# An attention and MLP mixer on one core: a second queue for one load, w4 products moved between units, and softmax sums sent by DMA instead of TensorE

## The chip, the core and the metric

The kernel runs on one core of a Trainium2 chip. A core has TensorE (PE, matrix products into PSUM), VectorE (DVE), ScalarE (ACT), GpSimd (POOL) and SyncE (SP), each with an instruction stream of its own that runs in order; they wait for each other by semaphores. DMAs are issued from the streams of SP, ACT and POOL. The metric is device time in microseconds of one execution. Times of the kernel before, three runs: 198.87, 199.20 and 199.33 us, median 199.2.

## What is computed

The input x has 2048 positions of 512 features. It is layer-normed, and two branches are formed from it:

```
xn = layernorm(x)
# A: attention, 32 heads of 16; position i looks at i, i-2, ..., i-14 (8 keys, step 2)
q, k, v = split(xn @ wqkv);  s = softmax(q.k / 4 over the 8 keys) . v  @ wo
# B: gated mixer
h  = gelu(layernorm(xn) @ w1);  hs = (h, four quarters shifted by 1, -1, 2, -2 positions) @ w2
x1 = xn + hs;  h2 = gelu(layernorm(x1) @ w3) @ w4       # w3: 512 x 1376
out = x + s * silu(x1 + h2)
```

All tensors are bf16, sums are taken in f32.

## The kernel before, in words

Since the keys of a position lie at even distances, even and odd positions never meet in the attention. They are kept as two halves, p = 0 and 1, of 1024 positions each, and each half is cut into 8 output tiles of 128 positions; tiles are numbered 0 to 15 over both.

**Front part (to about 103 us).** x is loaded in tiles of 128 positions (load_x, L115), normed on DVE and transposed, and q, k (qk, L283), w1, w2 and w3 follow for four chunks of 512 positions. The first loads are issued on SP in this order: x tiles 0 and 1, half of wqk, x tiles 2 and 3, the other half of wqk, then larger pieces of x.

**Units.** Attention is done in 17 units (list `order`, numbers 0 to 16). Unit 0 takes the first 64 positions of both halves, every other unit 128 keys and 112 to 120 queries of one half: units 1 to 8 half 0, units 9 to 16 half 1. A unit has these steps:
- scores (L593): 32 small products into the four PSUM banks "s";
- exps (L609): ACT takes the exponential of the whole score block, 128 x 2048;
- within (L617): DVE takes the minimum with a band of 0 and huge values, which clears what lies outside the 8 keys;
- weighted (L636), one unit later: 64 small products with the values, into the two banks "o". The values tile carries a constant 2.0 beside each head, so the rows of o_ps also hold twice the sum of the weights. DVE copies and adds the strip that the two blocks of 64 share (mix, L666, L667), and an eviction (ACT, L668) writes the rest to orw;
- values (L568): 4 products for the next unit into bank "b", evicted by ACT.

**w4 products.** Between these, TensorE multiplies h3 by w4, 11 products for each of the 16 tiles, into bank "w" (w4_part, L522). DVE adds x1 to the sum (L537). The gate is then made as x * (1 + tanh(x/2)), which is twice the silu: tanh on ACT (gate_tanh, L550), product on DVE (gate_mult, L558). Near the end the ACT table of Silu is loaded instead (L922), and gate_silu (L544) makes the gate in one step; the factor 2, which the doubled sums need, then comes in the final multiply.

**Sums.** Units are grouped in runs (L60): one unit, or two neighbours. The outputs of a run must be divided by its sums and brought from orw to the layout oT that the last product needs. There are two ways:
- by DMA: sums_gather (two DMAs on SP put the sums on 128 partitions), sums_invert (DVE reciprocal, then a DMA to DRAM), sums_read (a DMA that spreads them over all partitions, into orw), sums_apply (a multiply of oT). moves (L684) are eight DMAs, one for each group of heads, that carry orw to oT on SP's and POOL's queues;
- by TensorE: sums_turn (8 products, L703), sums_inverse (DVE reciprocal and two ACT copies), sums_back (4 products, L741), sums_mult (DVE, L750), and for the moves rows (8 products, L728, and an ACT copy).

Runs here are (0), (1,2), (3,4), ..., (11,12), (13), (14), (15), (16); the last three, 14, 15 and 16, go by TensorE (the moves of 14 by DMA).

**Output.** final (L789) multiplies oT of one tile with wo, 4 products into a bank (often "b", the one of values); a gate multiply on DVE (L813, L811) and an add of x follow (POOL, L818), and store (L843) writes two tiles. Tiles 0 to 7 of half 0 and tiles 0 and 1 of half 1 are done in units 6 to 15, the other six after the loop, the last two partly by TensorE (pe_add, L831).

**What sets the order.** Every engine's instructions stand in the order of the source: the last lines of the kernel bind each instruction to the one before it on its engine. So the order of the loop (L855 to L916) and of the lines after it (L917 to L961) is the order on each engine and queue. PSUM has eight banks; in the loop "s" holds four, "o" two, "w" and "b" one each, and after the loop the four of "s" become "f", "g", "h", "i".

Of the kernel before, what the change touches and what calls it, by code (L numbers as in the profile page):

```python
# [8 lines left out]
AF = mybir.ActivationFunctionType  # L9
# [6 lines left out]
def kernel(  # L16
# [19 lines left out]
    W = 8  # L36
    F = 1376
    ND = D // P
    NF = (F + P - 1) // P
# [3 lines left out]
    CH = 512  # L43
# [15 lines left out]
    NC = 3  # L59
    runs = [(0, 0)] + [(a, a + 1) for a in range(1, NN - NC - 1, 2)] + [(a, a) for a in range(NN - NC - 1, NN)]  # L60

# [53 lines left out]
    def load_x(c, n):  # L115
        p, k = c // 2, c % 2
        for t0 in range(k * TPC, (k + 1) * TPC, n):
            sp.dma_start(  # L118
                out=xn[p][:, t0 : t0 + n, :],
                in_=xv[p, t0 * P : (t0 + n) * P, :].rearrange("(i q) d -> q i d", q=P),  # L120
            )
            yield
# [513 lines left out]
    def weighted(n, first=lambda: None):  # L636
# [27 lines left out]
        first()  # L664
# [3 lines left out]
        return lambda: act.activation(wide(ow, c, KB, m), wide(ov_, 0, CH + W, m), AF.Copy)  # L668
# [83 lines left out]
    def sums_invert(i):  # L752
        _, a, b, _, rw, parts = run_of(runs[i][0])
        dn = rden[i]
        rb = small.tile([P, H * rw // P], BF16, name="rb", tag="rb")
        with nc.allow_low_precision("bf16 weights"):
            dve.reciprocal(out=rb, in_=dn)
        rden_d = dram.tile([8, ND * rw], BF16, name=f"rden_d{i}")
        sp.dma_start(out=rden_d.rearrange("h (a m) -> (h a) m", a=P // 8), in_=rb)
        rden[i] = rden_d  # L760
# [89 lines left out]
    CUT = 6  # L850
# [4 lines left out]
    for n in range(NN - 1):  # L855
        scores(n)
        back = [i for i, (a, b) in enumerate(runs) if b == n - 2 and i < R - NC]
        done = [i for i, (a, b) in enumerate(runs) if b == n - 1]
        evict = weighted(n - 1) if n > 0 else lambda: None
        for i in back:  # L860
            sums_invert(i)
        exps(n, 2 if n == 0 else 1)
        if n == NN - 2:
            values(n + 1)
        evict()
        if 0 < n < NN - 2:
            values(n + 1)
        gate_mult()
        if n < NN - 2:
            gate_tanh()  # L870
        for i in done:
            if i < R - NC:
                sums_gather(i)
        if n == 2:
            moves(0, [sp, pool], 1)
        for i in back:
            if 0 < i < R - NC - 1:
                moves(i, [sp], None, [6, 7])
            sums_read(i)
        for i in done:  # L880
            if i == 0:
                moves(i, [sp, pool], 0)
            elif i < R - NC - 1:
                moves(i, [pool, sp], None, range(6))
            elif i == R - NC - 1:
                moves(i, [pool], None, range(4))
            else:
                moves(i, [pool, sp])
        if n == NN - 2:
            store(sp, 0, 6)  # L890
        within(n, 2 if n == 0 else 1)
        late = [i for i, (a, b) in enumerate(runs) if n == max(b + 3, 5)]
        w4_part(n, 0, NF if n < NN - 2 else CUT)
        if n == 0:
            values(n + 1)
        gate = final(*final_at[n]) if n in final_at else None
        if n == NN - 2:
            banks["end"] = True
            sums_turn(R - 3, "o")
            sums_inverse(R - 3)  # L900
            for i in late:
                sums_apply(i)
        if gate:
            gate(pool)
        if n < NN - 2:
            for i in late:
                sums_apply(i)
        if n == NN - 3:
            moves(R - NC - 1, [pool], None, range(4, 8))
        if n % 2 == 0 and 10 <= n < NN - 3:  # L910
            load_xo((n - 2) // 8, (n - 2) % 8)
        if n - 1 in final_at and n % 2 == 0 and n < NN - 3:
            p, i = final_at[n - 1]
            store(sp, p, i - 1)
        if n in (10, 12):
            load_xo(1, n - 6)  # L916
    scores(NN - 1)  # L917
    evict = weighted(NN - 2)
    store(sp, 1, 0)
    exps(NN - 1)  # L920
    evict()
    act.preload_act_table_set("silu_and_others")  # L922
    w4_part(NN - 2, CUT, NF)
    gate_silu(NN - 2)
    within(NN - 1)
    gate2 = final(1, 2, "b")
    layout("high", f=1, g=1, h=1, i=1)
    sums_back(R - 3, "f")
    gate3 = final(1, 3, "h")
    sums_apply(R - 4, pool)  # L930
    evict = weighted(NN - 1, first=lambda: gate2(pool))
    evict()
    sums_turn(R - 2, "g")
    sums_inverse(R - 2, rows(R - 2, "i"), True)
    gate3(pool)
    store(sp, 1, 2)
    gate4 = final(1, 4, "w")
    sums_mult(R - 3)
    sums_turn(R - 1, "g")
    sums_back(R - 2, "f")  # L940
    sums_inverse(R - 1, rows(R - 1, "h"), True)
    sums_mult(R - 2)
    gate_silu(NN - 3)
    gate5 = final(1, 5, "b")
# [3 lines left out]
    sums_back(R - 1, "i")  # L948
    gate6 = final(1, 6, "g")
    sums_mult(R - 1)  # L950
# [3 lines left out]
    gate7 = final(1, 7, "fw", lambda: add6(gate6.sg))  # L954
# [47 lines left out]
```

## Time and profile before

| | us |
|---|---|
| median of three runs | 199.2 |
| profiled execution, its own time | 199.36 |
| span from first to last instruction in it | 197.6 |
| TensorE busy | 190.2 |
| ScalarE busy | 126.7 |
| VectorE busy | 125.1 |
| GpSimd busy | 61.8 |
| mean DMA rate | 113 GB/s |

The granted TensorE clock is 1.0 throughout. A busy TensorE is not one at its peak, since products overlap. In the timeline each line gives the start and the length in us, the engine, the line of the kernel, the operation, what it writes and reads, and how many were merged; a bracket tells how long the engine stood idle before and what released it. SPq is the issuing of DMAs by SP, PEld the loading of weights. A DMA's line is its issue; when its data has landed is seen only from who waits for it.

### The profile page before, as it was taken

To read this page: it belongs to the slowest core of one execution; us is meant where nothing else is said; L and a number is where in the kernel's file an instruction comes from. 1 tells how busy PE (TensorE), PEld (TensorE's weight loads), DVE (VectorE), ACT (ScalarE), POOL (GpSimd) and SP (SyncE) were. 2 spreads that over 40 slices of the span, in tenths; PEclk is the share of its full clock that TensorE was granted. 3 is DMA by queue.
4 is the path that set the end of the run, shared out by engine and by line. 5 is a ranking of instruction groups with operands and counts; after the bars stand their busy time and mean duration, and the time that the engine had idled before them with its cause. 6 is when DMAs were issued, how large, how long until landed. Compare 5 with 4: busy or idle time off the path is not lost.

```text
span 197.6 us, 6164 instructions
## 1 busy us (share of the span) xinstructions
PE 190.2 (96%) x2591; PEld 98.5 (50%) x2591; DVE 125.1 (63%) x249; ACT 126.7 (64%) x140; POOL 61.8 (31%) x114
## 2 busy tenths in 40 slices
PE   7699999999999999999999999999999999999991
PEld 2588844444444444444444555555555554546550
DVE  4788856418539968200004776788888887786892
ACT  3559849644830643556558788887666676667961
POOL 4135722810200220200000533032626242469760
PEclk9999999999999999999999999999999999999999
DMA  5982181389452256460330012222232271713333
GB/s 158 304 281 84 60 268 53 122 151 339 140 154 62 76 137 167 121 140 0 119 117 3 12 22 66 73 49 69 44 101 62 59 207 31 233 33 88 88 119 108
DMA packets 33643, 22.32 MB, mean 113 GB/s; under 512 B 17584, under 2 KB 33104, under 8 KB 33616
## 3 DMA queue, kind: packets, MB, share of 16 engines
q1 hardware_dynamic: 32256, 21.06, 37.5%
q0 software_dynamic: 1216, 0.81, 2.1%
q8 instruction: 20, 0.33, 0.7%
q10 hardware_dynamic: 144, 0.07, 0.1%
q14 instruction: 7, 0.06, 0.1%
HBM read 12.41 MB, written 4.83 MB: 87 GB/s over the span
## 4 chain that ended last, share of the span: by engine, by line
PE 91%; DMA 3%; DVE 2%; SPq 1%; issue 1%; ACT 1%; DVEq 0%
PE w_ps L529 19%; PE w_ps L394 18%; PE qk_ps L297 13%; PE v_ps L582 8%; PE w_ps L354 7%; PE w_ps L330 7%; PE wo_ps L802 6%; PE o_ps L650 6%; DMA wqk_sb<-in_A_wqkv_dram 3%; PE s_ps L603 3%; PE w_ps L410 1%; PE tr_ps L265 1%; SPq L118 1%; PE dt_ps L703 1%; DVE oT L750 1%
## 5 line engine op out<-in xcount | busy, mean ns | idle before, releaser
L614 ACT ACTIVATE prob<-s_ps 128x2048 bf16<-128x2048 f32 (+1 forms) x18 | 31.9, 1781 | 18.0 <-PE s_ps L603 17.9
L529 PE MATMUL w_ps<-w_sb,h3T 128*128 128x512 bf16 (+1 forms) x176 | 40.8, 379 | 0.0
L398 ACT ACTIVATE h3T<-w_ps 128x1024 bf16<-128x1024 f32 x20 | 20.5, 1023 | 24.9 <-PE w_ps L394 24.9
L693 POOL DMA_DIRECT2D oT<-orw x38 | 19.4, 518 | 49.9 <-DVE orw L658 30.3
L394 PE MATMUL w_ps<-x1nT,w_sb 128*128 128x512 bf16 x160 | 35.0, 379 | 0.0
L297 PE MATMUL qk_ps<-xnT,wqk_sb 128*128 128x256 bf16 (+1 forms) x192 | 29.7, 308 | 1.2 <-DMA wqk_sb<-in_A_wqkv_dram 0.7
L529 PEld LDWEIGHTS <-h3T 128*128 128x128 bf16 (+1 forms) x176 | 17.1, 98 | 20.4
L394 PEld LDWEIGHTS <-w_sb 128*128 128x128 bf16 x160 | 15.6, 98 | 19.1 <-issue 0.4
L297 PEld LDWEIGHTS <-wqk_sb 128*128 128x128 bf16 x192 | 18.3, 98 | 11.2 <-DMA wqk_sb<-in_A_wqkv_dram 1.0
L623 DVE TENSOR_TENSOR prob<-prob,band 128x2048 bf16<-128x2048 bf16 (+1 forms) x18 | 21.0, 1167 | 2.9 <-ACT prob L614 2.7
L304 ACT ACTIVATE qT<-qk_ps,sel 128x1024 bf16<-128x1024 f32 x16 | 16.7, 1113 | 6.6 <-PE qk_ps L297 6.5
L818 POOL TENSOR_TENSOR xo<-sg,xo 128x512 bf16<-128x512 bf16 x9 | 11.7, 1304 | 21.5 <-DVE sg L813 21.5
L802 PE MATMUL wo_ps<-wo_sb,oT 128*128 128x512 bf16 (+1 forms) x68 | 16.6, 366 | 0.1
L582 PE MATMUL v_ps<-wv_sb,xnT 128*128 128x512 bf16 x64 | 16.6, 381 | 0.0
L359 DVE TENSOR_TENSOR xn<-w_ps,xn 128x1024 bf16<-128x1024 f32 x8 | 9.7, 1212 | 10.6 <-PE w_ps L354 10.6
L537 DVE TENSOR_TENSOR xn<-w_ps,xn 128x512 bf16<-128x512 f32 x15 | 10.4, 691 | 7.6 <-PE w_ps L529 7.5
L585 DVE CAST v_aug<-v_ps 128x512 bf16<-128x512 f32 x1 | 0.7, 691 | 22.5 <-ACT h3T L398 22.5
L668 ACT ACTIVATE orw<-o_ps 128x896 bf16<-128x896 f32 x16 | 14.6, 913 | 0.1
L330 PE MATMUL w_ps<-xn2T,w_sb 128*128 128x512 bf16 x64 | 14.5, 379 | 0.0
L354 PE MATMUL w_ps<-w_sb,hT 128*128 128x512 bf16 x64 | 14.3, 379 | 0.0
L650 PE MATMUL o_ps<-prob,v_aug 64*32 64x64 bf16 x1088 | 12.2, 195 | 0.1
L334 ACT ACTIVATE hT<-w_ps 128x1024 bf16<-128x1024 f32 x8 | 8.2, 1028 | 6.2 <-PE w_ps L330 6.2
(100 smaller groups left out, 236.0 us busy)
## 6 DMA issues: line engine op xcount, KB each, us to landing
x1n_dram<-xn SPq DMA_DIRECT2D x4, 512.0 KB
xn<-in_A_x_dram SPq DMA_DIRECT2D x6, 256.0 KB
xo<-in_A_x_dram SPq DMA_DIRECT2D x6, 256.0 KB
out_dram<-xo SPq DMA_DIRECT2D x6, 256.0 KB
orw<-rden_d SPq DMA_DIRECT2D x6, 240.0 KB
w_sb<-in_B_w_dram SPq DMA_DIRECT2D x1, 1376.0 KB
w_sb<-in_B_w_dram SPq DMA_DIRECT2D x1, 1280.0 KB
wqk_sb<-in_A_wqkv_dram SPq DMA_DIRECT2D x2, 512.0 KB
```

Source lines behind the costliest of these rows:

```text
L297: pe.matmul(pt[:, b, :], lhsT=wqk_sb[:, dt, nt * P : (nt + 1) * P], rhs=xnT[p][:, dt, ms], start=(dt == 0), stop=(dt == ND - 1),)
L330: pe.matmul(pt[:, b, :], lhsT=w1_sb[:, dt, g * P : (g + 1) * P], rhs=xn2T[:, dt, :], start=(dt == 0), stop=(dt == ND - 1),)
L354: pe.matmul(pt[:, j, :], lhsT=w2_src(p, g, m0), rhs=w2_sb[:, g, :], start=(g == 0), stop=(g == ND - 1),)
L394: pe.matmul(pt[:, b, :], lhsT=w3_sb[:, dt, ft * P : (ft + 1) * P], rhs=x1nT[:, dt, :], start=(dt == 0), stop=(dt == ND - 1),)
L398: act.activation(h3_tile(c)[:, 2 * a : 2 * a + 2, :], pt, AF.Gelu_apprx_tanh)
L529: pe.matmul(pt, lhsT=h3[c][:fs, ft, jj * P : (jj + 1) * P], rhs=w4_sb[:fs, ft, :], start=(ft == 0), stop=(ft == NF - 1 and t < NN - 2),)
L582: pe.matmul(vp, lhsT=xnT[p][:, dt, k0 : k0 + P], rhs=wv_sb[:, dt, :], start=first, stop=last)
L614: act.activation(pr[:, rs_], t[:, rs_], AF.Exp, scale=SCALE)
L623: dve.tensor_tensor(out=w, in0=w, in1=b.unsqueeze(1).to_broadcast([P, m, KB]), op=ALU.min)
L650: pe.matmul(op[32 * cg : 32 * cg + 32, s, g * KB : (g + 1) * KB], lhsT=va[KB * s : KB * s + KB, dt * 8 + h, :], rhs=pr[KB * s : KB * s + K ...
L693: queues[hh % len(queues)].dma_start(out=oT[p][DH * hh : DH * (hh + 1), :, q0 : q0 + nq], in_=w[32 * cg : 32 * cg + DH, ND * jj : ND * jj ...
L802: pe.matmul(pt, lhsT=oT[p][:, dt, i * P : (i + 1) * P], rhs=wo_sb[:, dt, cs], start=(dt == 0), stop=(dt == ND - 1),)
```

## The change

Five things change together.
1. x tile 1 is issued by ACT's queue instead of SP's.
2. Units 1 to 6 take 7 or 8 w4 products each instead of 11; a tile may begin in one unit and end in the next. Units 7 to 15 take the whole tile n - 2. Tiles 14 and 15 are multiplied after the loop, tile 15 in bank "f". Tiles 12, 13 and 14 get their gate by Silu (before, tile 14 alone); tile 15 as before.
3. Runs are now (0), (1,2), ..., (13,14), (15), (16), and only run 16 goes by TensorE. Run 15's moves are issued after the loop, five on POOL and three on SP.
4. The eviction of o_ps of unit 15 is done by DVE instead of ACT.
5. In units up to 6 the reciprocal, the last two moves and the read of a run stand behind within; sums_apply of runs 0 and 1 stands ahead of within in unit 6 (before, behind the w4 products of unit 5).

```diff
-    NC = 3
-    runs = [(0, 0)] + [(a, a + 1) for a in range(1, NN - NC - 1, 2)] + [(a, a) for a in range(NN - NC - 1, NN)]
+    runs = [(0, 0)] + [(a, a + 1) for a in range(1, NN - 2, 2)] + [(a, a) for a in range(NN - 2, NN)]
...
-            sp.dma_start(
+            (act if (c, t0) == (0, 1) else sp).dma_start(
...
-        return lambda: act.activation(wide(ow, c, KB, m), wide(ov_, 0, CH + W, m), AF.Copy)
+        dst, src = wide(ow, c, KB, m), wide(ov_, 0, CH + W, m)
+        return lambda: act.activation(dst, src, AF.Copy) if eng is act else eng.tensor_copy(out=dst, in_=src)
...
+    part = {0: [(0, 0, NF)]}
+    for n in (1, 4):
+        t = 1 + (n - 1) // 3 * 2
+        part.update({n: [(t, 0, 7)], n + 1: [(t, 7, NF), (t + 1, 0, 3)], n + 2: [(t + 1, 3, NF)]})
+    part.update({n: [(n - 2, 0, NF)] for n in range(7, NN - 1)})
...
         evict = weighted(n - 1) if n > 0 else lambda: None
-        for i in back:
-            sums_invert(i)
+        if n > 6:
+            for i in back:
+                sums_invert(i)
         exps(n, 2 if n == 0 else 1)
...
         evict()
-        if 0 < n < NN - 2:
-            values(n + 1)
         gate_mult()
+        if len(part[n]) > 1:
+            w4_part(*part[n][0])
+        if n > 0:
+            values(n + 1)
...
+        if n == 6:
+            sums_apply(0)
+            sums_apply(1)
         within(n, 2 if n == 0 else 1)
+        if n <= 6:
+            for i in back:
+                sums_invert(i)
+            read_back()
...
-        w4_part(n, 0, NF if n < NN - 2 else CUT)
+        w4_part(*part[n][-1])
...
     scores(NN - 1)
-    evict = weighted(NN - 2)
-    store(sp, 1, 0)
+    evict = weighted(NN - 2, dve)
+    sums_invert(R - 3)
     exps(NN - 1)
     evict()
+    sums_gather(R - 2)
+    sums_read(R - 3)
+    moves(R - 2, [pool], None, range(5))
     act.preload_act_table_set("silu_and_others")
-    w4_part(NN - 2, CUT, NF)
-    gate_silu(NN - 2)
-    within(NN - 1)
-    gate2 = final(1, 2, "b")
-    layout("high", f=1, g=1, h=1, i=1)
-    sums_back(R - 3, "f")
-    gate3 = final(1, 3, "h")
-    sums_apply(R - 4, pool)
-    evict = weighted(NN - 1, first=lambda: gate2(pool))
-    evict()
-    sums_turn(R - 2, "g")
-    sums_inverse(R - 2, rows(R - 2, "i"), True)
-    gate3(pool)
-    store(sp, 1, 2)
-    gate4 = final(1, 4, "w")
-    sums_mult(R - 3)
-    sums_turn(R - 1, "g")
-    sums_back(R - 2, "f")
-    sums_inverse(R - 1, rows(R - 1, "h"), True)
-    sums_mult(R - 2)
-    gate_silu(NN - 3)
-    gate5 = final(1, 5, "b")
+    gate_mult()
+    within(NN - 1)
+    w4_part(NN - 3, 0, NF)
+    for t in range(NN - 5, NN - 2):
+        gate_silu(t)
+    gate2 = final(1, 2, "b")
+    gate2(pool)
+    sums_invert(R - 2)
+    moves(R - 2, [sp], None, range(5, 8))
+    sums_read(R - 2)
+    store(sp, 1, 0)
+    evict = weighted(NN - 1)
+    evict()
+    sums_apply(R - 3)
+    layout("high", f=1, g=1, h=1, i=1)
+    w4_part(NN - 2, 0, NF, "f")
+    gate_silu(NN - 2)
+    sums_turn(R - 1, "g")
+    sums_inverse(R - 1, rows(R - 1, "i"), True)
+    gate3 = final(1, 3, "b")
+    sums_back(R - 1, "g")
+    gate3(pool)
+    store(sp, 1, 2)
+    gate4 = final(1, 4, "h")
+    sums_mult(R - 1)
+    sums_apply(R - 2)
+    gate5 = final(1, 5, "w")
     gate4(pool)
     gate5(pool)
     store(sp, 1, 4)
-    sums_back(R - 1, "i")
-    gate6 = final(1, 6, "g")
-    sums_mult(R - 1)
+    gate6 = final(1, 6, "b")
```

Here R is the number of runs and NN = 17 that of units, so R - 1 is the run of unit 16, and after the change R - 2 is run 15 and R - 3 run (13,14). In the text "run 14" or "run 15" names a run by its unit.

## The prediction

> **What bounds the kernel now.** I read the engines' busy time first, then the chain that ended last, then the timeline of its three stretches: start, one attention unit, tail.
>
> ```profile
> PE 190.2 (96%) x2591; PEld 98.5 (50%) x2591; DVE 125.1 (63%) x249; ACT 126.7 (64%) x140; POOL 61.8 (31%) x114
> PE 91%; DMA 3%; DVE 2%; SPq 1%; issue 1%; ACT 1%; DVEq 0%
> ```
>
> TensorE is the chain from 9.29 us to about 193 us. Its work counts in full wherever it stands; moving it gains only where it fills a hole, and costs where it opens one. The timeline of the start, and of one early unit:
>
> ```profile
> 0.80 0.86 SPq L118 DMA_DIRECT2D xn<-in_A_x_dram  x2
> 1.70 0.43 SPq L128 DMA_DIRECT2D wqk_sb<-in_A_wqkv_dram  x1
> 9.29 1.05 PE L297 MATMUL qk_ps<-xnT,wqk_sb 128*128 128x256 bf16 x8 [0.74 <-DMA wqk_sb<-in_A_wqkv_dram]
> ...
> 116.84 0.43 PE L603 MATMUL s_ps<-qT,kT 32*64 32x128 bf16 x32
> 117.20 0.75 PE L650 MATMUL o_ps<-prob,v_aug 64*32 64x64 bf16 x64
> 117.37 1.88 ACT L614 ACTIVATE prob<-s_ps 128x2048 bf16<-128x2048 f32 x1 [0.61 <-PE s_ps L603]
> 118.04 0.22 DVE L666 COPY mix<-o_ps 128x64 f32<-128x64 f32 x1 [0.40 <-PE o_ps L650]
> 118.44 0.68 DVE L561 SCALAR_TENSOR_TENSOR xn<-sig,xn 128x512 bf16<-128x512 bf16 x1
> 119.28 1.23 DVE L623 TENSOR_TENSOR prob<-prob,band 128x2048 bf16<-128x2048 bf16 x1 [0.16 <-ACT prob L614]
> ```
>
> Scores start a unit; exps begin 0.55 us later and last 1.88, the band minimum follows with 1.22, and only then may the next unit's o_ps run. That is 3.7 us of latency inside a unit of 4.3, so it is hidden now, by 0.6 us. The tail:
>
> ```profile
> 181.54 0.43 PE L603 MATMUL s_ps<-qT,kT 32*64 32x128 bf16 x32
> 182.66 0.65 SPq L765 DMA_DIRECT2D orw<-rden_d  x1
> 183.36 2.61 SPq L693 DMA_DIRECT2D oT<-orw  x4
> 185.64 1.25 POOL L773 TENSOR_TENSOR oT<-oT,orw 128x480 bf16<-128x480 bf16 x1 [0.78 <-DMA orw<-rden_d]
> 189.99 1.35 DVE L813 TENSOR_TENSOR slots<-wo_ps,xn 128x512 bf16<-128x512 f32 x2
> 190.80 2.27 POOL L818 TENSOR_TENSOR slots<-slots 128x512 bf16<-128x512 bf16 x2 [1.40 <-PE wo_ps L802]
> 193.10 1.68 SPq L844 DMA_DIRECT2D out_dram<-slots  x3
> ```
>
> The reader should see that a read of reciprocals from DRAM takes 2.95 us from issue to use, and that the end is carried by the gates of output tiles 4 and 5: multiply at 189.99 on DVE, two adds on POOL, three stores on SP. I take A = the scores of unit 16 (181.54) and G = the multiply of gate 4 (189.99 = A + 8.45) as marks; from G to the span's end are 7.65 us.
>
> **The change, part by part, up to A.**
>
> *x tile 1.* SP issues x 0, x 1, wqk half 0 at 0.80, 1.25, 1.70; without x 1 all that follows is issued 0.45 earlier. The DMA share stays at 0.75 or more from 2.0 us nearly throughout to 13.5 (windows of 0.5 us), so the stream moves as a block and wqk half 1 lands 0.45 earlier, inside the 0.74 that TensorE waits. Tile 0 now shares the engines with tile 1 and can land up to 0.37 later (128 KB at about 350 GB/s); its chain to the first qk matmul then ends near 8.9 instead of 8.55. ScalarE's table load moves back by one issue, 0.45, to 2.5; its first root is at 3.94. Bounds 0 and -0.45; I take **-0.40**, nearer the issue slot, since no other wait follows on TensorE before 103 us.
>
> *Products moved behind A.* Before A stood 15 whole w4 tiles and 6 products, 171; now 14 tiles, 154. Eleven products take 2.38 us: 17 x 0.216 = **-3.68**, to come back in the tail. sums_turn of run 14 also leaves this stretch: **-0.41** (chain, L703 at 181.21).
>
> *Holes in units 1 to 6.* A unit shrinks to 0.36 + 0.61 + 0.97 + 7 x 0.216 = 3.45 us (3.67 with 8). ScalarE needs 1.77 + 0.80 + 0.48 + 0.53 = 3.58 with a tanh and 3.05 without (the steps between its starts at 113.07, 114.84, 115.64 and 116.12, and a tanh of 0.64 less an overlap of 0.11); four of six have one, so its mean of 3.40 just fits. DVE does not always. In units 2 and 5 one w4 tile ends and the next begins in the same PSUM bank, with only values (0.97) between. Measured from the scores: the mix copy at 1.31, gate_mult at 1.71, the w4 add at about 2.30 to 2.99 (0.69, L537); TensorE is ready for the new tile at 2.80 and starts at 3.06: 0.26. The band minimum follows the add, 2.91 to 4.13; o_ps wants to start at 4.07: 0.13. Twice 0.39 is **+0.78**. Units 1, 3 and 4 come out with 0.01 to 0.5 to spare.
>
> *Unit 7.* sums_apply of runs 0 and 1 now stands before the band minimum of unit 6 (1.07 us as at 130.73), which ends at 4.77 after that unit's scores. Behind it wait the reciprocal (0.44), the w4 add (0.61) and the first gate's multiply (0.69), so the multiply ends 1.75 us after unit 7's scores. values(8) needs that multiply's bank ("b") at 0.97 and starts at 1.82: **+0.85**. Before, this multiply stood at 135.30, 0.12 behind the scores, and ended in time. Nothing before shows either kind of hole; the low end is 0 for both (DVE's gaps smaller than its issue steps), the high end twice (a gate_mult beside POOL's add took 1.06 at 136.71 instead of 0.63).
>
> A therefore comes at 181.54 - 0.40 - 3.68 - 0.41 + 0.78 + 0.85 = **178.68**.
>
> **From A to G**, times counted from A. DVE: multiply 0.18, apply 0.78, mix 1.35, its add 1.60 (as unit 14 before: scores 171.75, then 171.93, 172.53, 173.10, 173.35), reciprocal of run (13,14) 1.74, then the copy of o_ps that ScalarE did: 1.07 long (L658's 1.225 x 896/1024), 2.18 to 3.25. Next on DVE the band minimum to 4.47; o_ps(16), wanted at 4.21, waits 0.33. Then the w4(14) add and gate 2, to 5.69.
>
> Run 15's sums start from that copy: two gathers on SP 3.28 to 4.5 (1.23 at 175.11). Landing after the issue: between 1.4 (moves on POOL's queue, 1.9 with 0.51 of issue) and 3.2 (issue end 170.87, reciprocal released 174.1, behind x loads); one at 121.25 was in by 122.94, so I take 1.4, no loads being ahead: 5.9. Reciprocal to 6.28, write issued to 6.8, three moves at 0.65 ahead of the read in SP's queue to 8.75, read at 8.8, landing 2.95 later: 11.75. sums_apply (half of 0.65) 11.8 to 12.15. Gate 4 stands behind it on DVE: **G = A + 12.15**, against 8.45. Its own wo_ps is ready at 10.97.
>
> TensorE in the meantime: w4(14) to 3.35, final(1,2) to 4.21, o_ps(16) to 5.15, w4(15) with its identity product to 7.75, turn and rows of run 16 to 8.55, final(1,3) to 9.4, a hole to 9.9 (the reciprocal on DVE waits behind the apply of run (13,14), whose 240 KB read, issued at 4.55, is in after 3.5; data of the one at 177.91 moved until 180.8), back, final(1,4) and (1,5) to 11.83. The 22 products thus fill the first 8 us, and the sums of two runs that no longer pass through TensorE (0.41 + 0.54 + 2 x 0.21 + 0.33 = 1.70 us) are not missed: SP's loop ends last. The mix copy of unit 16 waits behind the DMA-fed reciprocal (6.3), and ScalarE's eviction behind it ends at 7.75, just when TensorE asks. ScalarE's table load and three Silu (1.28 + 3 x 0.6) end by 5.8, before that eviction at 6.85.
>
> Past G the order is the old one (gates 4, 5 on DVE, POOL, three stores), so 7.65 stays; final(1,6) waits to 12.2 and the last ScalarE store falls at 15.4, before SP's last.
>
> The Trainium skill, "DMA: Bandwidth & Descriptors", section "Anatomy of one DMA", gives about 2.0 us plus bytes/436e3 per us for a GpSimd-issued DMA: 2.28 for a read of this size (an estimate from that page). The read above took 2.95, with a queue behind it; by the page's figure the sum would be 199.4 instead of 200.0.
>
> **Sum.** G = 178.68 + 12.15 = 190.83, 0.84 later than 189.99. The profiled execution took 199.36 (span 197.6 and 1.7 around it): 200.2, and it lies 0.16 above the median of the runs: **200.0**.
>
> **Rivals.**
> - *Loop lands sooner.* If the read is in by A + 11.1, DVE is just done with the multiply of run 16 (11.0) and G falls 0.65 earlier: about 199.35. For it: part of the 2.95 may be the four moves queued behind that read. Against: the windows show its data moving only 1.3 to 2.35 us after issue. The skill's 2.0 us leans this way.
> - *No holes in the loop (faster).* If DVE's order leaves units 2, 5 and 7 unharmed, 1.63 us return: 198.4. It turns faster than before once the holes are under 0.4 together. For it: DVE shows 1 to 2 us idle per unit now. Against: the idle is not where the waits fall.
> - *More holes.* If band minimum and exps bind each of the six short units (they have 0.1 us of slack, and POOL's work stretches DVE's), 0.2 to 0.3 each: 201.3.
> - *x tile 1 gains nothing* (wqk half 1 is bound by the stream): 200.4, inside my case.
>
> **Numbers.** Forecast case 0.45 (199.65 to 200.8), sooner 0.17, no holes 0.18, more holes 0.20. About 0.2%, 0.4 us, is what a measurement of this kernel can tell. The no-hole case gives faster, with a little of the sooner case: 0.21; same: most of the sooner case and the forecast's low edge, 0.19; slower 0.60. Range 198.6 to 201.3.
>
> **What the profile after would show.** TensorE's wait for wqk gone or under 0.3 us; PE idle on DVE at the third products of units 2 and 5 and at values in unit 7; A near 178.7; the reciprocal of run 15 waiting for its gather; DVE idle before its last sums_apply, released by the DMA orw<-rden_d; G near 190.8. I am wrong if A is below 178 (holes absent), or if the last apply doesn't wait.

## The result, and the profile after

The changed kernel takes 204.52 us (median of 5 executions, 202.97 to 205.05) against 199.2 us before: a ratio of 1.026, 95% interval 1.022 to 1.031. It is slower by 5.3 us, where 0.8 us had been forecast; 204.5 lies far above the range of 198.6 to 201.3. The profiled execution took 204.8, with a span of 203.1 us (before: 197.6).

The page of the changed kernel, engines' busy time and the chain that ended last:

```profile
PE 190.5 (94%) x2533; PEld 97.7 (48%) x2559; DVE 124.1 (61%) x247; ACT 124.5 (61%) x134; POOL 59.2 (29%) x110
PE 70%; DMA 10%; DVE 6%; ACT 5%; issue 3%; SPq 3%; ACTq 0%
```

TensorE is busy for as long as before, though it has 1.7 us less to do, and its share of the chain has fallen from 91% to 70%. DMA has gone from 3% to 10%. The kernel has stopped being one long row of products. Two stretches of the timeline show where. The first is units 6 and 7 of the changed kernel (start, length, engine, line, operation, and in brackets the idle time before it and what ended that):

```profile
126.21 0.64 SPq L765 DMA_DIRECT2D orw<-rden_d  x1
126.42 0.43 PE L603 MATMUL s_ps<-qT,kT 32*64 32x128 bf16 x32
...
130.39 0.66 DVE L773 TENSOR_TENSOR oT<-oT,orw 128x960 bf16<-128x960 bf16 x1 [1.00 <-DMA oT<-orw]
130.97 1.22 DVE L623 TENSOR_TENSOR prob<-prob,band 128x2048 bf16<-128x2048 bf16 x1
131.11 1.04 PE L802 MATMUL wo_ps<-wo_sb,oT 128*128 128x512 bf16 x4 [0.77 <-DVE oT L773]
132.08 0.43 PE L603 MATMUL s_ps<-qT,kT 32*64 32x128 bf16 x32
...
133.82 1.02 PE L582 MATMUL v_ps<-wv_sb,xnT 128*128 128x512 bf16 x3 [0.70 <-DVE sg L813]
```

The read of run (1,2)'s reciprocals is issued at 126.21 and its multiply runs 4.18 us later, after DVE has waited 1.00 us. final(0,0) waits behind it. At 133.82 is the wait in unit 7 that the prediction had named. The second stretch is the tail:

```profile
180.46 0.43 PE L603 MATMUL s_ps<-qT,kT 32*64 32x128 bf16 x32
185.25 0.61 SPq L765 DMA_DIRECT2D orw<-rden_d  x1
187.09 2.94 SPq L693 DMA_DIRECT2D oT<-orw  x3
190.64 0.66 DVE L773 TENSOR_TENSOR oT<-oT,orw 128x960 bf16<-128x960 bf16 x1 [3.61 <-DMA oT<-orw]
190.76 0.64 SPq L765 DMA_DIRECT2D orw<-rden_d  x1
192.37 0.38 PE L741 MATMUL rr_ps<-ident,slots 120*128 120x120 bf16 x4 [2.28 <-ACT slots L716]
192.81 4.44 PE L802 MATMUL wo_ps<-wo_sb,oT 128*128 128x512 bf16 x12
192.86 0.66 DVE L750 TENSOR_TENSOR oT<-rr_ps,oT 128x480 bf16<-128x480 f32 x1 [0.75 <-ACT oT L733]
194.04 0.41 DVE L773 TENSOR_TENSOR oT<-oT,orw 128x480 bf16<-128x480 bf16 x1 [0.52 <-DMA orw<-rden_d]
194.51 0.69 DVE L811 SCALAR_TENSOR_TENSOR slots<-wo_ps,xn 128x512 bf16<-128x512 f32 x1
196.22 0.69 DVE L811 SCALAR_TENSOR_TENSOR slots<-wo_ps,xn 128x512 bf16<-128x512 f32 x1 [1.01 <-PE wo_ps L802]
```

The multiply of run (13,14) keeps DVE waiting for 3.61 us; it runs 5.39 us after its read was issued. Run 16's reciprocal stands behind it on DVE, and TensorE needs that one for sums_back, so TensorE stands for 2.3 us. Only behind sums_back come the multiply of run 16 (192.86) and run 15's (194.04). The 12 products after the hole take 4.44 us instead of 2.6. The windows of the changed kernel say why (columns: stretch, its length, busy time of PE, PEld, DVE, ACT, POOL with instruction counts, then the granted TensorE clock, the DMA share and GB/s):

```profile
193.00:194.00 1.00, 1.00 (x4) 0.41 (x3) 0.52 (x1) 0.00 (x0) 0.34 (x1) 0.52 0.59 203
194.00:195.00 1.00, 1.00 (x4) 0.29 (x2) 0.89 (x2) 0.00 (x0) 0.00 (x0) 0.50 0.68 245
195.00:196.00 1.00, 1.00 (x4) 0.31 (x3) 0.21 (x1) 0.00 (x0) 0.71 (x1) 0.50 0.06 17
196.00:197.00 1.00, 1.00 (x5) 0.45 (x4) 0.69 (x1) 0.00 (x0) 0.44 (x2) 0.78 0.00 0
```

The granted clock is 0.50 for 3.4 us: from about 193.04 (0.52 in its window) to 196.44 (0.78 in its window). Before, it was 1.0 throughout.

The marks A (scores of unit 16), G (the multiply of gate 4) and the end give the sum:

| | before | forecast | after |
|---|---|---|---|
| scores of unit 1 | 108.21 | 107.81 | 107.92 |
| A | 181.54 | 178.68 | 180.46 |
| A to G | 8.45 | 12.15 | 14.05 |
| G to end of span | 7.65 | 7.65 | 8.6 |
| span | 197.6 | 198.5 | 203.1 |

As a ledger of the 5.5 us: unit 1 begins 0.29 earlier, and the sums taken from TensorE give -1.70 (0.41 of it before A); new waits before A cost +3.30 (A would stand at 177.16 without them: 181.54 - 0.29 - 3.68 - 0.41), and the tail costs +4.16. The tail, and unit 6 before A, have one thing in common: DVE waits for a transfer, and TensorE for DVE. The experiments test how much of the loss that is.

### The profile page after: what moved, and what is told of

It reads as the page before. It is cut to its first block, busy times and chain, and to the rows that moved or that the text cites. A ratio compares the mean times of both kernels' runs of the same rounds, so it can differ in the third digit from the quotient of the medians.

```text
span 203.1 us, 6062 instructions
## 1 busy us (share of the span) xinstructions
PE 190.5 (94%) x2533; PEld 97.7 (48%) x2559; DVE 124.1 (61%) x247; ACT 124.5 (61%) x134; POOL 59.2 (29%) x110
## 4 chain that ended last, share of the span: by engine, by line
PE 70%; DMA 10%; DVE 6%; ACT 5%; issue 3%; SPq 3%; ACTq 0%
PE w_ps L394 17%; PE qk_ps L297 14%; PE w_ps L529 8%; PE w_ps L354 7%; PE w_ps L330 7%; DMA oT<-orw 5%; PE wo_ps L802 5%; PE v_ps L582 5%; PE o_ps L650 3%; SPq L679 2%; ACT orw L668 2%; PE s_ps L603 2%; DMA dn<-orw 2%; DMA rden_d<-rb 2%; ACT v_aug L587 2%
## 5 line engine op out<-in xcount | busy, mean ns | idle before, releaser
L398 ACT ACTIVATE h3T<-w_ps 128x1024 bf16<-128x1024 f32 x20 | 20.5, 1023 | 24.9 <-PE w_ps L394 24.9
L693 POOL DMA_DIRECT2D oT<-orw x35 | 17.9, 519 | 47.8 <-DVE orw L658 30.3
L529 PEld LDWEIGHTS <-h3T 128*128 128x128 bf16 (+1 forms) x176 | 16.8, 98 | 20.6 <-issue 0.9
L623 DVE TENSOR_TENSOR prob<-prob,band 128x2048 bf16<-128x2048 bf16 (+1 forms) x18 | 21.1, 1173 | 3.4 <-ACT prob L614 3.4
L818 POOL TENSOR_TENSOR xo<-sg,xo 128x512 bf16<-128x512 bf16 x10 | 12.9, 1289 | 27.6 <-DVE sg L813 27.6
L304 ACT ACTIVATE qT<-qk_ps,sel 128x1024 bf16<-128x1024 f32 x16 | 16.7, 1112 | 6.6 <-PE qk_ps L297 6.5
L802 PE MATMUL wo_ps<-wo_sb,oT 128*128 128x512 bf16 (+1 forms) x68 | 18.0, 396 | 1.0 <-DVE oT L773 0.8
L582 PE MATMUL v_ps<-wv_sb,xnT 128*128 128x512 bf16 x51 | 15.9, 381 | 1.4 <-DVE sg L813 0.7
L668 ACT ACTIVATE orw<-o_ps 128x896 bf16<-128x896 f32 x15 | 13.7, 913 | 1.8 <-DVE orw L666 1.8
L650 PE MATMUL o_ps<-prob,v_aug 64*32 64x64 bf16 x1088 | 12.9, 196 | 0.0
```

What stands on the lines that cost most here:

```text
L398: act.activation(h3_tile(c)[:, 2 * a : 2 * a + 2, :], pt, AF.Gelu_apprx_tanh)
L529: pe.matmul(pt, lhsT=h3[c][:fs, ft, jj * P : (jj + 1) * P], rhs=w4_sb[:fs, ft, :], start=(ft == 0), stop=(ft == NF - 1 and t < NN - 2),)
L582: pe.matmul(vp, lhsT=xnT[p][:, dt, k0 : k0 + P], rhs=wv_sb[:, dt, :], start=first, stop=last)
L623: dve.tensor_tensor(out=w, in0=w, in1=b.unsqueeze(1).to_broadcast([P, m, KB]), op=ALU.min)
L650: pe.matmul(op[32 * cg : 32 * cg + 32, s, g * KB : (g + 1) * KB], lhsT=va[KB * s : KB * s + KB, dt * 8 + h, :], rhs=pr[KB * s : KB * s + K ...
L693: queues[hh % len(queues)].dma_start(out=oT[p][DH * hh : DH * (hh + 1), :, q0 : q0 + nq], in_=w[32 * cg : 32 * cg + DH, ND * jj : ND * jj ...
```

## The experiments

Theory 1: the chain of DMAs that carries a run's sums (gather, write, read back) has a latency of its own, and its last step, the read, is needed sooner than it lands once units last 3.5 us, and at the tail. DVE runs in order, so it holds everything behind the waiting multiply. Rivals: DVE's and ScalarE's own work is too long for short units; the tail is bound by run 15's loop alone; the half clock is a cause and not a consequence. Part 5 of the change, the new order in units up to 6, was not tried alone. The interval of each ratio is against the kernel before, whose median was 199.1 to 199.5 beside these runs.

### The parts alone

**x tile 1 alone.** The kernel before, with x tile 1 on ACT's queue.

```diff
-            sp.dma_start(
+            (act if (c, t0) == (0, 1) else sp).dma_start(
```

> The kernel before with one part of the change alone: x tile 1 issued by ScalarE's queue. In the changed kernel unit 1's scores began 0.29 us earlier (107.92 instead of 108.21), although tile 0 landed 0.63 us later. If that is a gain of its own, nothing behind it eats it: 198.9 (198.8 to 199.0). If it is lost in a later wait of the old order: 199.2.

Measured: 199.36 us, ratio 1.001 (0.999 to 1.003): no change. Lines of this run's timeline:

```profile
174.69 0.53 DVE L757 RECIPROCAL rb<-dn 128x60 bf16<-128x60 bf16 x1 [1.51 <-DMA dn<-orw]
...
183.86 0.66 DVE L773 TENSOR_TENSOR oT<-oT,orw 128x960 bf16<-128x960 bf16 x1 [1.74 <-DMA rden_d<-rb]
```

Unit 1 starts 0.13 earlier than before (108.08 against 108.21), unit 15 0.51 earlier (176.54 against 177.05), and unit 16 0.12 later. The gather of run (11,12) is waited for 1.51 us instead of 0.55, and the last multiply of the loop 1.74 instead of 0.35. So a lead of half a us can be lost to DVE's waits for transfers. But the profiled execution took 200.77 us, the longest of the twelve: where the others, near 199.4, lose the gain, or whether they have one, isn't shown.

**The products alone.** The kernel before, with the w4 products in the units of the changed one; the sums of runs 14 to 16 stay on TensorE.

```diff
-    CUT = 6
+    part = {0: [(0, 0, NF)]}
+    for n in (1, 4):
...
-        w4_part(n, 0, NF if n < NN - 2 else CUT)
+        w4_part(*part[n][-1])
```

> The kernel before with the products moved as in the change (7 or 8 in units 1 to 6, tiles 14 and 15 after the loop), but loads, runs and sums as before (14, 15 and 16 through TensorE). Theory 1: no loop of DMAs in the tail, so only the holes of units 2 and 5 (0.48 and 0.45 in the changed kernel) and some in units 6 and 7 remain, against at most 0.9 of holes filled in the tail: 199.5 to 201. Theory 2: most of the loss stays: 203 or more.

Measured: 201.67 us, ratio 1.013 (1.010 to 1.016), 2.4 us slower and above what was expected. The tail is what it was (A to end 19.6, before 16.1 + 3.68 moved = 19.8); A comes at 179.72, some 2 us later than without waits. Four lines of its units 2 to 6:

```profile
114.65 0.81 PE L529 MATMUL w_ps<-w_sb,h3T 128*128 128x512 bf16 x3 [0.38 <-DVE xn L537]
122.19 0.53 DVE L757 RECIPROCAL rb<-dn 128x60 bf16<-128x60 bf16 x1 [1.32 <-DMA dn<-orw]
123.85 0.68 PE L650 MATMUL o_ps<-prob,v_aug 64*32 64x64 bf16 x64 [0.70 <-DVE prob L623]
128.81 0.66 DVE L773 TENSOR_TENSOR oT<-oT,orw 128x960 bf16<-128x960 bf16 x1 [0.92 <-DMA dn<-orw]
```

Only the first is a wait for an engine's own work. At 122.19 the reciprocal waits for its gather, the band minimum stands behind it, and o_ps behind that; at 128.81 the multiply of run (1,2) waits again, 4.23 us after its read (the line names a gather; that the read is meant is inferred). Since TensorE had no hole before, moving products had nothing to fill, and the shorter units opened holes.

**Sums (and x tile 1), without the products.** The changed kernel with every w4 tile whole in its own unit, as before.

```diff
-    part = {0: [(0, 0, NF)]}
...
+    part = {n: [(n, 0, NF)] for n in range(NN - 1)}
-    w4_part(NN - 3, 0, NF)
...
-    w4_part(NN - 2, 0, NF, "f")
```

> The changed kernel with the w4 products put back (tile n whole in unit n, tile 15 in unit 15, none after the loop); loads and sums as changed. Theory 1, the sums' DMA loop after the loop sets the end: the marks A (scores of unit 16) comes near 182.1, from A to the end it takes as long as in the changed kernel (22.6 us) or a little more, TensorE's hole grows by the 5 us that the products filled, and the time is 205 to 207. Theory 2, the holes that the moved products open in units 2 to 8 are the loss: without them 200 or less.

Measured: 205.16 us, ratio 1.030 (1.027 to 1.033). Now the tail has nothing to put into the DMA loop's time. Its timeline, and one of its windows:

```profile
187.67 0.74 PE L650 MATMUL o_ps<-prob,v_aug 64*32 64x64 bf16 x64 [1.92 <-DVE prob L623]
190.92 0.96 PE L703 MATMUL dt_ps<-ident,orw 128*120 128x4 bf16 x8 [2.50 <-ACT orw L668]
192.21 0.66 DVE L773 TENSOR_TENSOR oT<-oT,orw 128x960 bf16<-128x960 bf16 x1 [2.38 <-DMA oT<-orw]
```

```profile
190.00:191.00 1.00, 0.08 (x1) 0.08 (x2) 0.00 (x0) 1.00 (x2) 0.48 (x1) 0.50 0.59 180
```

TensorE does hardly anything from 186 to 190.9, and the clock is halved for some 6.8 us around it. A comes at 183.23, 1.1 later than expected, and the end 20.6 us behind it instead of 22.6: the time is as expected, the marks are not. So the products cost 2.4 us alone, all the rest 5.9, and both together 5.3: the moved products fill part of the time for which the sums' loop leaves TensorE idle. The 5.9 holds part 5 too. By it run (3,4)'s reciprocal stands behind the band minimum of unit 6: it runs 4.83 us after that unit's scores, and the multiply of (3,4) then waits 1.56 us. With the products alone, where part 5 is absent, these are 2.64 us and no wait. What part 5 costs by itself is open.

### The tail

**Run 15 through TensorE.** The changed kernel, with runs 15 and 16 through TensorE and (13,14) by DMA.

```diff
-    sums_gather(R - 2)
-    sums_invert(R - 2)
-    sums_read(R - 2)
-    sums_apply(R - 3)
...
+    sums_turn(R - 2, "g")
+    sums_inverse(R - 2, rows(R - 2, "i"), True)
...
+    sums_back(R - 2, "h")
     sums_inverse(R - 1, rows(R - 1, "i"), True)
...
+    sums_apply(R - 3)
```

> The changed kernel with run 15's sums through TensorE again; run (13,14) still by DMA, all else as changed. Theory 1 in its narrow form, the three steps of run 15's loop (gather, write, read behind the moves) set the end: gate 4's multiply comes at about A + 11 instead of 14.05, no long hole in TensorE, granted clock 1.0 to the end: 200.5 to 202. If the read for run (13,14), 5.4 us from issue to use, is enough by itself to hold VectorE and TensorE: 203 to 204.

Measured: 203.95 us, ratio 1.024 (1.021 to 1.026): the time of the second expectation, but not its cause. Taking run 15's loop away gives no more than about half a us. Lines of its timeline, with the clock at 1.0:

```profile
185.05 0.65 SPq L765 DMA_DIRECT2D orw<-rden_d  x1
190.71 0.36 DVE L711 RECIPROCAL rbt<-dt_ps 120x32 bf16<-120x32 f32 x1 [1.34 <-PE dt_ps L703]
191.53 0.65 DVE L773 TENSOR_TENSOR oT<-oT,orw 128x960 bf16<-128x960 bf16 x1
192.46 0.81 PE L802 MATMUL wo_ps<-wo_sb,oT 128*128 128x512 bf16 x3 [1.22 <-DVE oT L773]
```

TensorE waits 1.22 us for the multiply of run (13,14). But that multiply runs 6.48 us after its read was issued, without a wait of its own: the edit has put it behind run 16's reciprocal on DVE (190.71), which waits 1.34 us for TensorE. So this run doesn't test whether the read of (13,14) alone would hold the tail; its order has a hole of another kind. A to end is 20.5 us, against 22.6; A comes 0.35 later, as unit 6 takes 6.30 us in this execution.

**The late read not waited for.** The changed kernel; one multiply takes a constant operand.

```diff
+    FREE = (R - 3,)
+        if i in FREE:
+            rr = wo_sb[:, :, 0:rw]
```

> The changed kernel, with the sums_apply of run (13,14) multiplying by a constant tile instead of the reciprocals read back from DRAM; the read itself is still issued, so those 30 columns of queries are left undivided. Theory 1 (the 3.61 us for which DVE waits for that 240 KB read holds reciprocal(16), and by it TensorE, and the half clock follows from that hole): DVE doesn't wait at 187 to 190.6, sums_back comes at about A+9.5 instead of A+11.9, the hole at 190 is gone; run 15's loop is untouched, so gate 4 still comes at A+13.6 to 14.0, and only the 0.95 behind it and part of the half clock return: 203.2 to 204.0. TensorE will then wait for sums_apply(15) ahead of final(1,6), about 3 us; if that hole halves the clock too, nothing returns: 204.3. Rival (run 15's loop is late only because DVE is held): gate 4 at A+12.2 as first predicted, 202.3 or less.

Measured: 203.53 us, ratio 1.021 (1.017 to 1.024), about 1 us less than the changed kernel. Its timeline:

```profile
187.12 1.02 DVE L776 TENSOR_TENSOR oT<-oT,wo_sb 128x960 bf16<-128x960 bf16 x1
189.94 0.39 PE L742 MATMUL rr_ps<-ident,slots 120*128 120x120 bf16 x4
193.70 0.41 DVE L776 TENSOR_TENSOR oT<-oT,orw 128x480 bf16<-128x480 bf16 x1 [2.37 <-DMA orw<-rden_d]
194.03 2.29 DVE L814 SCALAR_TENSOR_TENSOR slots<-wo_ps,xn 128x512 bf16<-128x512 f32 x4
194.16 1.04 PE L805 MATMUL wo_ps<-wo_sb,oT 128*128 128x512 bf16 x4 [1.91 <-DVE oT L776]
```

The multiply still depends on its run's moves and doesn't wait, so the 3.61 us were the read's, although the profile's line names a move. TensorE's hole at 190 is gone; but run 15's multiply now waits 2.37 us for its own read, G falls at A + 13.6 (180.41 here), and A to end is 21.5. With the first read out of the way the second holds the end: that is why removing the first brings so little. Nor would a punctual read of run 15 alone bring much: in the changed kernel DVE is busy with run 16's multiply until 193.52, 0.52 us before run 15's begins (an estimate from its lines). The rival "run 15's loop is late only because DVE is held" (G at A + 12.2) is wrong.

**The hole filled.** The changed kernel with 12 products that nothing reads, ahead of the last sums_back.

```diff
+    fill = pst("w", "fill_ps")[:, 0, :]
+    for _ in range(12):
+        pe.matmul(fill, lhsT=ident[:], rhs=wo_sb[:, 0, :], start=True, stop=True)
     sums_back(R - 1, "g")
```

> The changed kernel with 12 products more (identity by a weight tile into an unused bank, never read) placed ahead of the last sums_back, where TensorE stands idle for 2.4 us; they take about 2.6 us. Theory 1 (the granted clock halves because TensorE stood idle there): the clock stays near 1.0 from 193 to 196.4, the 12 wo products take 2.6 us instead of 4.44, gate 5 comes 0.9 sooner, G to end goes from 8.6 back to about 7.65: 203.4 to 203.8 (sums_back itself may come 0.2 later). Rival (the clock halves for another reason, or the products behind the hole are off the path): 204.4 to 204.8, clock 0.5 as before or the end unmoved.

Measured: 204.22 us, ratio 1.022 (1.018 to 1.026), not told apart from the changed kernel in time. In its profile the tail runs at 1.0 and takes 21.2 us from A instead of 22.6. That is what the clock theory asks for, but it doesn't test it: in this execution the read of run (13,14) was used after 4.15 us instead of 5.39, so that the products filled a hole that would have been about 1.1 us long (an estimate: TensorE is free at 190.84, run 16's reciprocals are ready at 191.93). The half clock has struck elsewhere in the same execution, in unit 6, as its timeline and one window show:

```profile
131.33 0.66 DVE L773 TENSOR_TENSOR oT<-oT,orw 128x960 bf16<-128x960 bf16 x1 [2.37 <-DMA oT<-orw]
132.04 1.61 PE L802 MATMUL wo_ps<-wo_sb,oT 128*128 128x512 bf16 x4 [1.95 <-DVE oT L773]
```

```profile
133.00:134.00 1.00, 1.00 (x34) 0.41 (x32) 1.00 (x3) 0.00 (x0) 0.00 (x0) 0.50 0.00 0
```

Nothing was edited there: this time the read of run (1,2) was issued 0.56 later and waited for 2.37 us instead of 1.00, and four products of final(0,0) took 1.61 instead of 1.04.

### The early units

**The early read not waited for.** The edit of the run before last, with run (1,2) instead.

```diff
+    FREE = (1,)
```

> The changed kernel, with the sums_apply of run (1,2) multiplying by a constant tile instead of its reciprocals (the read is still issued; those queries are left undivided). Theory 1 (unit 6 is 1.13 longer because sums_apply(1) waits 1.00 us on DVE for its 240 KB read): unit 6 at about 3.5 us instead of 5.66 less its own added work, A 1.0 to 1.3 sooner, 203.2 to 203.5. Rival 1 (DVE's own order of work there is too long, the wait only fills a gap): unchanged, 204.3 to 204.6. Rival 2 (the hole moves on to unit 7 or 8, whose reads are as late): 0.3 to 0.6 sooner, 203.9 to 204.2.

Measured: 201.47 us, ratio 1.011 (1.008 to 1.014): 3 us less than the changed kernel, more than any theory had. Unit 6 falls from 5.66 to 4.77 us (scores at 126.43 and 131.20), A to 179.35, 1.1 earlier, as theory 1 expected. The rest is in the tail, where the profiled execution still has the hole:

```profile
189.32 0.66 DVE L776 TENSOR_TENSOR oT<-oT,orw 128x960 bf16<-128x960 bf16 x1 [3.24 <-DMA oT<-orw]
...
191.05 0.58 PE L742 MATMUL rr_ps<-ident,slots 120*128 120x120 bf16 x4 [1.98 <-ACT slots L717]
191.49 4.11 PE L805 MATMUL wo_ps<-wo_sb,oT 128*128 128x512 bf16 x12
```

G is at A + 14.04, as in the changed kernel. But here the half clock begins at 190.9, earlier against G than there, is over at 194.3, and G to end is 7.3 instead of 8.6. The median gains once more, as only two of six executions show a mean clock of 0.991, with 202.4 us; the four at 0.994 to 1.0 took 201.0 to 201.5. Of the changed kernel four of five are at 0.992 or less (204.5 to 205.1), one at 0.998 (202.97). How much of the 3 us is the read and how much the luck of the clock isn't settled by six executions; against that one execution of 202.97 it is 1.5 to 2. Nor is the clock the only thing that varies: with later tiles (below) four executions at 0.998 to 1.0 took 201.1 to 203.3.

**The first part's add first.** In units 2 and 5 the add that frees the w4 bank is put ahead of gate_mult.

```diff
-        gate_mult()
         if len(part[n]) > 1:
             w4_part(*part[n][0])
+        gate_mult()
```

> The changed kernel, with the add of the first w4 part placed ahead of gate_mult on DVE (in units 2 and 5 that part ends one w4 tile, whose PSUM bank the next tile wants). Theory 1 (the holes of 0.48 and 0.45 in units 2 and 5 are the wait for that bank behind gate_mult): both shrink to 0.1 or less, A 0.7 to 0.9 sooner, 203.6 to 203.9. Rival (they are the band minimum's, which stands behind both in either order): the third product's wait goes, o_ps waits the longer, 204.3 to 204.7.

Measured: 204.02 us, ratio 1.024 (1.020 to 1.027), not told apart. Units 2 and 5 fall from 3.93 and 3.90 to 3.68 and 3.54 us, and units 3 and 6 rise by 0.55 and 0.50; A stays at 180.46. The line of unit 3 of this run:

```profile
115.81 0.68 PE L650 MATMUL o_ps<-prob,v_aug 64*32 64x64 bf16 x64 [0.57 <-DVE prob L623]
```

The rival was right for unit 3: the wait for the bank goes, and o_ps waits for the band minimum instead. In unit 6 the multiply of run (1,2) waits for its read as before, until 130.59 (130.39 in the changed kernel).

The tail of this profile, which the edit doesn't touch, is of more use. Here the read of run (13,14), issued at 185.50, was used after 3.85 us:

```profile
189.35 0.66 DVE L773 TENSOR_TENSOR oT<-oT,orw 128x960 bf16<-128x960 bf16 x1 [2.04 <-DMA oT<-orw]
191.08 0.38 PE L741 MATMUL rr_ps<-ident,slots 120*128 120x120 bf16 x4 [0.78 <-DVE slots L813]
193.47 0.41 DVE L773 TENSOR_TENSOR oT<-oT,orw 128x480 bf16<-128x480 bf16 x1 [1.24 <-DMA orw<-rden_d]
```

TensorE's hole is 0.78 us instead of 2.28, the clock stays at 1.0 without any added product, and A to end is 21.2 us, as in the run with the hole filled. Still G comes only at A + 13.3, as run 15's multiply now waits 1.24 us for its own read.

**Output tiles one unit later.** Each tile of the loop a unit later, the multiplies of runs 0 and (1,2) behind the band minimum of unit 6, and tile (1,1) in the tail.

```diff
-    final_at = {n: divmod(n - 6, 8) for n in range(6, 16)}
+    final_at = {n: divmod(n - 7, 8) for n in range(7, 16)}
...
     evict = weighted(NN - 1)
     evict()
+    gate1 = final(1, 1, "b")
+    gate1(pool)
```

> The changed kernel with all output tiles of the loop one unit later (tile (0,0) in unit 7 instead of 6, and so on), sums_apply of runs 0 and (1,2) at the end of unit 6 behind the band minimum, and tile (1,1) in the tail behind o_ps(16); the whole result is computed. Theory 1 (the reads of reciprocals are used sooner than they land, 3.9 to 5.4 us after their issue, once units take 3.5 us): unit 6 falls to about 3.6 plus no output tile, units 7 and 8 lose most of their 0.75 and 0.33, A = 180.46 - 0.86 (tile moved) - 1.1 - 0.7 = 177.8; the 1.04 of tile (1,1) fills part of the 2.4 us hole in the tail, A to end about 21.0; span 198.8, time 200.3 to 201.3. Rival (the holes come from DVE's and ScalarE's own work): they appear one unit later, A at 179.2 to 179.6 (only the moved tile gone), time 203 or more.

Measured: 202.50 us, ratio 1.016 (1.011 to 1.020), 2 us less than the changed kernel, but short of the expectation. Unit 6 falls to 3.70 us, as expected without a wait. Then the chain's other links wait; from this run's timeline:

```profile
131.13 0.53 DVE L757 RECIPROCAL rb<-dn 128x60 bf16<-128x60 bf16 x1 [1.09 <-DMA dn<-orw]
...
138.21 0.66 DVE L773 TENSOR_TENSOR oT<-oT,orw 128x960 bf16<-128x960 bf16 x1 [1.34 <-DMA oT<-orw]
...
191.45 0.38 PE L741 MATMUL rr_ps<-ident,slots 120*128 120x120 bf16 x4 [1.70 <-ACT slots L716]
```

Unit 7 takes 6.06 and unit 8 5.68 us, against 5.18 without waits; A comes at 178.85, midway between the two expectations. So neither is right alone: part of the wait goes, part moves on to the gather and the next read.

**Output tiles later, add first, run 15 through TensorE.** Three of the edits above at once.

```diff
-    final_at = {n: divmod(n - 6, 8) for n in range(6, 16)}
+    final_at = {n: divmod(n - 7, 8) for n in range(7, 16)}
...
-        gate_mult()
         if len(part[n]) > 1:
             w4_part(*part[n][0])
+        gate_mult()
...
+    sums_turn(R - 2, "g")
+    sums_back(R - 2, "h")
```

> The changed kernel with three edits at once, the whole result computed: output tiles one unit later (as in the run before the last), the first w4 part's add ahead of gate_mult, and run 15's sums through TensorE. Theory 1: A at 177.3 to 177.8; in the tail the hole of 1.2 us is filled by tile (1,1), A to end 20.0 to 20.7; 199.3 to 200.2, no slower than the kernel before by more than 0.5%. Rival (tail holes move on instead of filling): A to end 21.4 or more, 201 or more.

Measured: 202.77 us, ratio 1.018 (1.014 to 1.022): by its time the rival, while A to end, 21.1, lies between the two. The tail's hole isn't filled: tile (1,1) is through TensorE by 186.3, long before the hole, and at 192.74 TensorE still waits 1.23 us for the multiply of (13,14), which again stands behind run 16's reciprocal on DVE and not behind its read. A is at 179.66 (unit 8 takes 6.21 us). No combination that was tried beats the kernel before.

### All reads at once

The changed kernel with every multiply but run 0's taking the constant operand.

```diff
+        if i > 0:
+            rr = wo_sb[:, :, 0:rw]
```

> The changed kernel with every sums_apply but that of run 0 multiplying by a constant tile instead of the reciprocals read from DRAM (all DMAs are still issued; those queries are left undivided). Theory 1 (waits for these reads carry nearly all that the change lost): A at 178.2 to 178.6 (holes of units 2, 5 and 7 stay), no DVE wait in the tail, TensorE without a hole, full clock, A to end 18.5 to 19.2 as TensorE's own work (16.1 + 3.68 - 1.29 = 18.5); 198.4 to 199.6. Rival (the tail stays bound by DVE's, SP's and ScalarE's own order): A to end above 20.3 as in the run whose apply of (13,14) didn't wait, less 0.8, and 200.5 or more.

Measured: 200.12 us, ratio 1.0045 (1.0027 to 1.0063). Multiplies that wait for a read, with the gather and the write ahead of it, thus carry 4.4 of the 5.3 us, the half clock among them. No window of this run shows a clock under 1.0 while TensorE works. From its timeline:

```profile
131.46 0.53 DVE L757 RECIPROCAL rb<-dn 128x60 bf16<-128x60 bf16 x1 [0.97 <-DMA dn<-orw]
133.18 1.02 PE L582 MATMUL v_ps<-wv_sb,xnT 128*128 128x512 bf16 x3 [1.22 <-DVE sg L815]
...
189.48 0.38 PE L741 MATMUL rr_ps<-ident,slots 120*128 120x120 bf16 x4
191.73 2.29 DVE L813 SCALAR_TENSOR_TENSOR slots<-wo_ps,xn 128x512 bf16<-128x512 f32 x4
```

sums_back runs without a hole, G falls at A + 12.2 and A to end is 19.3. A, at 179.50, is later than expected: as unit 6 is shorter, run (3,4)'s gather is waited for 0.97 us, and values(8) waits 1.22 instead of 0.70. So of the 4.4 us only 0.96 are won before A, and 3.35 behind it (A to end was 22.6). Before A some 2.3 of the 3.30 us of waits stay. They are not the reads'; those followed here are the gathers' and DVE's order.

## Why the prediction was wrong

**Direction and first terms.** Slower was right, and the 17 products and the turn of run 14 went as counted. The holes in units 2 and 5 came to 0.48 and 0.45 us (0.39 each forecast), and the one in unit 7 to 0.75 (0.85). At the start unit 1 began 0.29 earlier where 0.40 was taken. TensorE's wait for wqk is gone, as forecast; its first product starts 0.63 later (7.21 against 6.58), where 0.37 had been allowed. That the load gives the 0.29 isn't shown: with the products alone, where x tile 1 stands on SP as before, the wait for wqk was 0.20 us instead of 0.74, and unit 1 began at 107.81.

**Unit 6, the first step that failed.** The prediction let sums_apply of runs 0 and 1 end 4.77 us after unit 6's scores, band minimum included, on 1.07 us of work, as if their data were there. The band minimum ended 5.77 after the scores (132.19): DVE waited 1.00 us for the read. That unit lost 1.13, unit 8 another 0.33 by the next read, units 9 to 12 0.1 to 0.2 each (some 0.6 of such small waits before had too: from 107.92, units of 3.45, 3.67 and 5.18 us without any add up to 176.5, not 177.16). The start (0.11) and 1.67 of holes more than forecast are the 1.78 by which A was missed. The rival "more holes" had the direction and gave the work of DVE and ScalarE as the cause. Before A both have a share: with the reads gone (the last run above) A came 0.96 earlier, more than half of the 1.67, but the gather of (3,4) and values(8) were then waited for longer.

**The size of a read, the term behind both failures.** "In after 3.5" for 240 KB was worked out from the windows, from where data stopped moving (180.8). What counts is when the waiting instruction runs. In the profile of before that read is issued at 177.91 and its multiply runs at 182.36 after a wait of 0.35: 4.45 us, if the wait was the read's (the line names a move, as it does in the changed kernel, where it was the read). In the runs here, where DVE waited, it took 3.85 to 5.4 us. At 5.4 the read of run (13,14) held DVE until A + 10.2, run 16's reciprocal behind it, and TensorE from 9.6 to 11.9 instead of 9.4 to 9.9.

**A to G: 14.05 for 12.15.** The prediction let run 15's loop alone set G. Up to the issue of its write that loop went as forecast: its reciprocal ended at 6.23 (6.28 forecast). Three moves on SP then took 2.94 instead of 1.95 us and SP waited 0.5 for the write, so the read left at 10.30 instead of 8.8; it was used 3.28 later instead of 2.95 (2.98 by the lines that the prediction shows). That would be the 1.90 by itself. But a second path was as late: the multiply of run 16, forecast to be done by 11.0, ended at A + 13.1, because its reciprocal had stood behind the multiply of (13,14). Run 15's lateness thus decides only the last half us. With the first wait taken away G was still at A + 13.6, with all reads taken away at A + 12.2, where the forecast had it. The Trainium skill's figure, "DMA: Bandwidth & Descriptors", section "Anatomy of one DMA", makes 2.28 of such a read (an estimate from that page, whose fit is for DMAs issued by GpSimd); the run of the changed kernel gives 3.28, so its lean towards the earlier landing was wrong here.

**G to end: 8.6 for 7.65.** That the stretch behind G stays as it was held in order but not in clock. A halved clock stood in no case of the prediction. It made gate 5 wait 1.01 us for its product. From G to the end of POOL's last add it took 3.63 us instead of 3.08; in three profiles whose tail ran at full clock (late read free, hole filled, add first) it took 3.0. So about 0.6 of the 0.95 goes with the clock. The rest lies between the issue of SP's last stores and the end of the span, 4.9 us instead of 4.5, and its cause is open.

**What would have shown it.** The signs given for being wrong (A below 178, or a last multiply that doesn't wait) were not the ones that came. The prediction asked whether DVE and ScalarE have time for a unit of 3.5 us; it should have asked the same of the chain gather, reciprocal, write, read, multiply, which doesn't get shorter when the units do. The gain side was small from the start: 1.70 us of sums, and at most the 0.74 us for which TensorE waited at its start.

## What to carry to other kernels

Before shortening the steps of a loop, list every transfer that is issued in one step and used in another, take its time from its issue to the instruction that waited for it (not to where its data stops moving), and compare it with the new step. A DMA round trip that replaces work of the bound engine can win only as long as nothing that engine needs stands behind the round trip on another engine's queue. Where several waits lie beside each other, take them all away at once to see their sum, since taken one at a time each can be covered by the next.

## What the runs showed of the hardware

The granted clock fell to 0.50 after short holes, each time for about 3.4 us (from the windows' means: 193.04 to 196.44 in the changed kernel, 132.36 to 135.78 with the filled hole, 190.86 to 194.28 with the early read free, 192.16 to 195.58 with later tiles; about 6.8 without the products, from 188.96 on, with little work from 186 to 190.9). Each began between 0.2 us before and 0.7 us after the end of a hole, of 2.28, 1.95, 1.98 and 1.70 us in the first four; holes of 1.91 us (the late read free, ahead of 194.16), 1.56 and 1.22 us (run 15 through TensorE, units 6 and tail) and 0.78 us (add first) were not followed by it. So the length of the hole alone doesn't decide; that the hole is what brings the half clock on is argued from these times, as no run changed the hole alone. Executions of one kernel differ: 202.97 us at a mean clock of 0.998, 204.5 to 205.1 at 0.987 to 0.992. The Trainium skill, "TensorE: Matmul & The Clock Gate", section "What's actually happening" in Part 1, has a free-running window of about 3.4 us that decides on the clock, with half speed after an idle one. The length of each stretch agrees with that, and holes of like length with and without it would fit a free-running window; that a hole of half such a window can be enough is what these runs add.

The 240 KB read of run (13,14) took 3.85, 4.15, 4.24, 5.0, 5.0 and 5.4 us from issue to use in the tails of six of these kernels, with nothing changed about it. What sets the difference was not tried.
